# Moving work between the branches of a switched expert loop, with the gate on another engine

## The chip, the core and the metric

The kernel runs on one core of one Trainium2 chip. The metric is device time in microseconds (us) for one launch; three runs of the kernel before gave 488.0, 491.76 and 497.99, and their median counts. Engines are named TensorE (PE in the profile; PEld is its weight load), VectorE (DVE), ScalarE (ACT), GpSimd (POOL) and SyncE (SP, which here only issues transfers).

## The reference

A recurrent attention block is followed by a mixture of experts in which each token goes to one expert. All data are 32-bit floats.

```python
# q, k, v: (4, 8, 768, 64)
state = zeros(B, H, D, D)
for t in range(S):
    state = gamma[h] * state + outer(k[:, :, t], v[:, :, t])
    y[:, :, t] = scale * q[:, :, t] @ state
x = y.transpose(0, 2, 1, 3).reshape(3072, 512)

idx  = argmax(x @ w_gate, axis=1)               # 8 experts
gate = softmax(x @ w_gate)[idx]
for e in range(8):                              # w1: 512 x 1024, w2: 1024 x 512 per expert
    rows = idx == e
    y[rows] = maximum(x[rows] @ w1[e], 0) @ w2[e]
out = gate[:, None] * y
```

How many tokens an expert has is known only on the chip.

## The kernel before

Up to about 150 us the kernel runs the attention block and the routing; the change does not touch how that is done, but for where some registers are loaded. Then come eight **jobs**, one for each expert, 0 to 7. Job 0 and a first part of job 1 (256 tokens, `EARLY`) are done apart. A job takes its tokens, transposed, in `xTs` (512 features by up to `W` = 512 tokens), multiplies by `w1`, takes the positive part into `hT` (1024 features), and multiplies by `w2` into `yT`.

**Arms.** A job's width is a number of tokens in steps of 8. `tc.Switch(which, ARMS, ...)` holds 33 bodies, the **arms**, one for each width from 256 to 512, and a register that was loaded from the counts picks one. TensorE, ScalarE and VectorE have instructions in the arms of jobs 1 to 7 and so branch there; GpSimd and SyncE have none and run straight through. `regs` loads the register on each branching engine (it shows as line 515, `TENSOR_LOAD arm`). `fetch_ahead` (line 519) is a hint to TensorE and ScalarE, not to VectorE, which arm the next Switch will take. Between two arms lies what is here called a **seam**: the engine leaves one arm, loads the register, and enters the next.

**The two layers.** Each layer is computed as seven products of quarters instead of eight, on half the job's width: tokens are split in two interleaved halves, so every product has `n // 2` columns, and sums and differences of operands and of results replace the eighth product. For a job: `S` (four tiles, the sums of quarters of `w1`, line 283) and `Z` (the same of `w2`, line 299) are made by GpSimd; `T` (sums of `xTs`, line 315) and `G` (sums of `hT`, line 381) by VectorE. `quarters1` (products at line 333) runs twice seven products, for two pairs of f; in each pair the order is ya, yb, yd, yc, ya, yd, yc. ya, yb, yc, yd are accumulators; after the first ya ScalarE copies it to `m1` (line 345); VectorE then adds yb to m1 into `u2`, yd to u2 into `u3` (line 337), and further results to these. The second ya, yd, yc products add to the buffers that hold the first ones. `quarters2` (products at line 395, adds at line 399) is the same for layer 2: A(0,0) and A(0,1), then Sq(2), Sq(3), Sq(1), and as its **last two products** A(1,1) by `G[3]` into yd and Sq(4) into yc.

**Between the products.** `spare1` in layer 1 has VectorE turn the former job's `yT` back into rows (`turn_back`, line 444); `spare2` in layer 2 has it turn the next job's tokens into `xTs` (line 438) and make `T`.

**At the seam, outside the arms**, in program order: `finish(e - 1)` sends the former job's rows from `yg` to `o` by SyncE (`exchange`, line 433, 16 transfers), GpSimd multiplies them by the gate (line 1125, four instructions) and scatters them to the output (line 500, four indirect transfers). Then GpSimd makes `S` for the next job, SyncE loads `w1` for the job after it (2 MB), exchanges that job's tokens and loads its `w2` (2 MB), and GpSimd gathers tokens of the third next job (line 171) and makes `Z`. Each engine runs its own stream in this order, held by semaphores where it needs another's result; so GpSimd makes S for the next job while TensorE is in the arm of the present one. After job 7 its remaining part (256 tokens) is done by `pair` (lines 455 to 484), with no Switch.

## Time and profile before

| | |
|---|---|
| Runs | 488.0, 491.76, 497.99 us; median 491.76 us |
| Profiled execution | 487.66 us, of it 485.9 us span |
| Mean granted TensorE clock | 0.951 |
| Busy, share of the span | TensorE 89%, VectorE 51%, ScalarE 24%, GpSimd 61% |
| TensorE idle ahead of line 333 | 35.2 us, 28.4 of it "issue" |
| GpSimd's gate, line 1125 | 45.4 us in 24 instructions |
| S on GpSimd, line 283 | 2.3 us for each of four |
| Instructions fetched (queues q8, q14) | 48 and 68 packets, 0.79 and 0.56 MB |

A row of a timeline has the start in us, the duration, engine, line, operation, the written tile and the read ones, and in brackets how long the engine stood idle before and what ended it. "issue" stands where it waited for nothing that the profile shows. A row of the groups ends with busy us, mean ns of one instruction, and the idle time ahead of the group with its main releaser. A row of the waits gives the total, how often, and the longest. The rows of TensorE with "x8" are one product for two f (f0 and f0 + 1), those with "x16" one product of layer 2 for both d, and "x32" the two ya products of layer 2; the number behind "128x" is the half width of the job. Jobs 1 to 7 had 196, 196, 212, 176, 208, 180 and 204 columns here.

### The profile page before, as it was taken

How to read it: one execution, taken by the hardware profiler on the slowest of the kernel's cores; microseconds unless marked ns; L12 is line 12 of the kernel's file. 1: busy time of each engine (PE TensorE's matmuls, PEld its weight loads, DVE VectorE, ACT ScalarE, POOL GpSimd, SP SyncE). 2: the span in 40 equal slices, each digit the busy share in tenths (PEclk: the TensorE clock that was granted, in tenths of full speed). 3: DMA queues.
4: the chain of work that ended last, by engine and by line, in shares of the span. 5: the costliest groups of instructions: out<-in, count | busy, mean ns of one | idle time of the engine just before them, and what ended most of it. 6: DMA issues, size and time to landing. Idle time of an engine off the chain costs nothing.

```text
span 485.9 us, 9701 instructions
## 1 busy us (share of the span) xinstructions
PE 430.5 (89%) x3595; PEld 394.1 (81%) x3595; DVE 246.9 (51%) x554; ACT 115.9 (24%) x269; POOL 296.8 (61%) x224
## 2 busy tenths in 40 slices
PE   6899999996999999859978996799599959959993
PEld 4688888885888699859968996799599859959872
DVE  4445768694689505424833482356067415815510
ACT  3355544542212122003201310130023003102310
POOL 3575545505073294257799599929996990797451
PEclk9999999997999999979997999799899979999997
DMA  9999999999414747948667457448746543011221
GB/s 198 237 230 212 236 239 211 231 240 375 122 41 128 288 113 238 396 88 275 209 180 236 92 206 211 144 94 280 229 120 206 154 172 77 27 62 39 52 87 48
DMA packets 122116, 85.33 MB, mean 176 GB/s; under 512 B 56970, under 2 KB 106122, under 8 KB 122000
## 3 DMA queue, kind: packets, MB, share of 16 engines
q1 hardware_dynamic: 116736, 71.34, 54.1%
q0 software_dynamic: 5120, 12.60, 7.8%
q8 instruction: 48, 0.79, 0.7%
q14 instruction: 68, 0.56, 0.4%
q10 hardware_dynamic: 144, 0.05, 0.0%
HBM read 60.88 MB, written 14.68 MB: 156 GB/s over the span
## 4 chain that ended last, share of the span: by engine, by line
PE 59%; DMA 13%; SPq 11%; issue 8%; DVE 5%; POOL 1%; ACT 1%; POOLq 0%; DVEq 0%; ACTq 0%
PE p L333 21%; PE p L395 8%; SPq L433 7%; PE p L230 6%; DMA w1t<-in_moe_w_dram 5%; PE y L681 4%; PE p L243 3%; PE hp L230 3%; PE sc L627 3%; DMA k<-in_k_dram 3%; PE p L455 2%; DMA w2t<-in_moe_w_dram 2%; DMA xs<-xs 2%; SPq L576 2%; PE trq L595 2%
## 5 line engine op out<-in xcount | busy, mean ns | idle before, releaser
L333 PE MATMUL p<-xTs,w1t 128*128 128x196 f32 (+5 forms) x192 | 44.1, 382 | 35.2 <-issue 28.4
L1125 POOL TENSOR_SCALAR o<-o,gate 128x512 f32<-128x512 f32 x24 | 45.4, 1904 | 46.2 <-DMA o<-o 27.7
L333 PEld LDWEIGHTS p<-xTs,w1t 128*128 128x128 f32 x192 | 38.5, 223 | 37.0 <-issue 36.8
L444 DVE STREAM_TRANSPOSE o<-yT 128x512 f32<-128x512 f32 x24 | 16.8, 699 | 59.4 <-issue 28.9
L171 POOL DMA_INDIRECT xs<-x_d,src x28 | 30.5, 1088 | 26.0 <-issue 12.6
L631 DVE TENSOR_TENSOR am<-sc,causal 128x512 f32<-128x512 f32 x48 | 30.0, 684 | 20.0 <-PE sc L627 19.9
L589 POOL TENSOR_TENSOR vs<-v,dec 128x512 f32<-128x512 f32 x23 | 25.3, 1117 | 23.7 <-DMA v<-in_v_dram 21.7
L333 PE MATMUL p<-t,s 128*128 128x196 f32 (+5 forms) x192 | 39.6, 354 | 0.0
L345 ACT COPY q<-p 128x196 f32<-128x196 f32 (+5 forms) x24 | 7.7, 322 | 130.1 <-PE p L333 130.1
L337 DVE TENSOR_TENSOR hT<-p,q 128x196 f32<-128x196 f32 (+5 forms) x72 | 25.2, 356 | 26.0 <-PE p L333 25.8
L500 POOL DMA_INDIRECT out_dram<-o,dst x26 | 27.3, 1052 | 16.3 <-ACT o L251 9.5
L333 PEld LDWEIGHTS p<-t,s 128*128 128x128 f32 x192 | 36.9, 212 | 0.2
L333 PE MATMUL p<-t,w1t 128*128 128x196 f32 (+5 forms) x192 | 35.8, 329 | 0.0
L395 PE MATMUL p<-g,w2t 128*128 128x196 f32 (+4 forms) x192 | 33.6, 328 | 0.0
L395 PE MATMUL p<-g,z 128*128 128x196 f32 (+4 forms) x192 | 33.6, 328 | 0.0
L584 POOL TENSOR_TENSOR qs<-q,dec 128x512 f32<-128x512 f32 x22 | 22.3, 1042 | 17.3 <-DMA q<-in_q_dram 15.6
L395 PE MATMUL p<-hT,w2t 128*128 128x196 f32 (+4 forms) x192 | 32.6, 328 | 0.0
L333 PEld LDWEIGHTS p<-t,w1t 128*128 128x128 f32 x192 | 32.6, 191 | 0.0
L395 PEld LDWEIGHTS p<-g,z 128*128 128x128 f32 x192 | 31.9, 190 | 0.0
L395 PEld LDWEIGHTS p<-g,w2t 128*128 128x128 f32 x192 | 31.9, 190 | 0.0
L395 PEld LDWEIGHTS p<-hT,w2t 128*128 128x128 f32 x192 | 31.7, 190 | 0.0
L681 PE MATMUL y<-am,vs 128*64 128x128 f32 x384 | 25.3, 286 | 3.8 <-POOL vs L589 3.8
(217 smaller groups left out, 856.9 us busy)
## 6 DMA issues: line engine op xcount, KB each, us to landing
w1t<-in_moe_w_dram SPq DMA_DIRECT2D x7, 2048.0 KB
w2t<-in_moe_w_dram SPq DMA_DIRECT2D x7, 2048.0 KB
k<-in_k_dram SPq DMA_DIRECT2D x24, 256.0 KB
v<-in_v_dram SPq DMA_DIRECT2D x24, 256.0 KB
x_d<-xg SPq DMA_DIRECT2D x48, 128.0 KB
xs<-xs SPq DMA_DIRECT2D x96, 64.0 KB
o<-o SPq DMA_DIRECT2D x96, 64.0 KB
q<-in_q_dram SPq DMA_DIRECT2D x11, 512.0 KB
```

Source lines behind the costliest of these rows:

```text
L171: nc.gpsimd.indirect_dma_start(out=xs[:, t, :], out_offset=None, in_=x_d[0:rows, :], in_offset=bass.IndirectOffsetOnAxis(ap=idx[:, t : t + ...
L230: nc.tensor.matmul(hp, lhsT=w1t[:, 0, dt, ts(f, P)], rhs=xT[:, dt, n0:n], start=(dt == 0), stop=(dt == DT - 1))
L333: nc.tensor.matmul(rows(y), lhsT=a(d, f), rhs=b(d), start=start and d == 0, stop=d == 1, skip_group_check=True)
L337: nc.vector.tensor_tensor(out=to, in0=rows(y), in1=rows(plus), op=ALU.add)
L395: nc.tensor.matmul(rows(y), lhsT=a(f, d), rhs=b(f), start=start and f == 0, stop=f == FH - 1, skip_group_check=True)
L433: nc.sync.dma_start(to[ts(g, L), :, ts(r, P)], got[ts(r, L), :, ts(g, P)])
L500: done = nc.gpsimd.indirect_dma_start(out=out[:, :], out_offset=bass.IndirectOffsetOnAxis(ap=idx[:, t : t + 1], axis=0), in_=o[:, t, :], i ...
L584: by.tensor_tensor(out=qs[:, e, part, :], in0=got[:, part, ts(e, D)], op=ALU.mult, in1=inner(dec[:, ts(2 * where[s][0] + e, H)][:, part], D))
L589: by.tensor_tensor(out=vs, in0=raw.pop(("v", s, b)), op=ALU.mult, in1=inner(dec[:, ts(NC + 2 * where[s][0] + where[s][2], H)], D))
L631: nc.vector.tensor_tensor(out=am[j], in0=sc[j], in1=middle(causal[:, :], HP), op=ALU.mult)
L681: nc.tensor.matmul(place_of(y, b, a, j), lhsT=vs[:, 2 * a + j, :], rhs=am[b][0][j][:, a, :], start=alone, stop=True, skip_group_check=True)
L1125: nc.gpsimd.tensor_scalar(out=yg[:, t, :].rearrange("p (a g l) -> p a g l", g=Q, l=L), in0=o[:, t, :].rearrange("p (g a l) -> p a g l", g= ...
```

## The change

A constant `SEAM` of 216 columns is introduced, and the products take a range of columns `c`.

- The last two products of layer 2, with their adds, leave the arm: `last2` runs them after the Switch for columns 0 to 216, whatever the width, and the arm only what lies above 216 (nothing for jobs of up to 432 tokens).
- The first product of the next job's layer 1, for both f, and its copy to `m1` (`first1`) leave the next arm in the same way and stand behind `last2`.
- The gate moves from GpSimd to ScalarE, as an activation with a scale.
- The registers of jobs 2 to 7 are loaded in the layer-1 loop of job 1 (f = 1 to 6), not one at each seam; that of job 1 is loaded behind the one of job 0.
- The hint for the next Switch stands behind the arm, ahead of `last2`, not ahead of layer 2 within the arm. Job 1's stays where it was.
- On GpSimd a copy of one column of `T[3]` into `turn_of` is put ahead of `S`, so `S` starts after `T[3]` is made; and the gather stands behind `Z`. The clearing of `yT` is cut to its upper columns, and those of `hT`, `G[3]` and `u2` are cleared as well, since the fixed width reads past the job's.

```diff
+    SEAM = 216
+    def last2(hT, w2t, S, T, yT, temps, c):
+        yc, yd = (acc8[i : i + 2] for i in (2, 4))
+        u2 = temps[1]
+        Y = lambda i, k, d: part_of(yT[:, 2 * i + d, :], k, c)
         for d in range(2):
-            product(yd[d], A(1, 1), Tq(4), d, False)
-            add(Y(1, 0, d), yd[d], u2[d])
+            products(yd[d], [(quarter_of_w2(w2t, 1, 1)[:, f, ts(d, P)], columns(T[3][:, f, :], c)) for f in range(FH)],
+                     c, False)
+            adds(Y(1, 0, d), columns(yd[d], c), columns(u2[d], c))
         for d in range(2):
-            product(yc[d], Sq(4), X(1, 1), d, False)
-            add(Y(0, 1, d), yc[d], u2[d])
+            products(yc[d], [(S[3][:, f, ts(d, P)], part_of(hT[:, FH + f, :], 1, c)) for f in range(FH)], c, False)
+            adds(Y(0, 1, d), columns(yc[d], c), columns(u2[d], c))
...
+    def first1(xT, w1t, f, ya, m1, c):
+        products(ya, [(w1t[:, 0, d, ts(f, P)], part_of(xT[:, d, :], 0, c)) for d in range(2)], c, c[0] == 0)
+        nc.scalar.copy(out=m1[:, c[0] : c[1]], in_=ya[:, c[0] : c[1]])
...
             for t in range(TC):
-                nc.gpsimd.tensor_scalar(out=yg[:, t, :].rearrange("p (a g l) -> p a g l", g=Q, l=L),
-                                        in0=o[:, t, :].rearrange("p (g a l) -> p a g l", g=Q, l=L),
-                                        scalar1=cols[e][2][:, t : t + 1], scalar2=None, op0=ALU.mult)
+                nc.scalar.activation(out=yg[:, t, :].rearrange("p (a g l) -> p a g l", g=Q, l=L),
+                                     in_=o[:, t, :].rearrange("p (g a l) -> p a g l", g=Q, l=L), func=AF.Copy,
+                                     scale=cols[e][2][:, t : t + 1])
             scatter(yg, cols[e][1], range(TC))
...
+        for f in range(FT):
+            layer1(EARLY, xT1, w1s[1], hT, f, banks=(2, 3, 4, 5, 0, 1))
+            if f == 0:
+                fetch_ahead(which[1], 1)
+            elif f < E - 1:
+                which[f + 1] = regs(f + 1)
...
-                fetch_ahead(nxt, e + 1)
-                quarters2(n, hT, w2s[e], Z, G, yT, temps, spare2)
+                quarters2(hT, w2s[e], Z, G, yT, temps, spare2, (0, n // 2))
+                if n // 2 > SEAM:
+                    last2(hT, w2s[e], Z, G, yT, temps, (SEAM, n // 2))
...
             if e > 1:
                 finish(e - 1)
-            S = halves_of_w1(w1s[e + 1], s3)
+            fetch_ahead(which[e + 1], e + 1)
+            last2(hT, w2s[e], Z, G, yT, temps, (0, SEAM))
+            for f in range(2):
+                first1(xTs, w1s[e + 1], f, acc8[6 + f], temps[0][f], (0, SEAM))
             if e + 2 < E:
                 w1s.append(weights1(homes[e % 2], e + 2))
                 exchange(xg, xs)
                 w2s.append(weights2(homes[e % 2], e + 2))
-            if e + 3 < E:
-                gather(xs, cols[e + 3][0], range(TC))
+            nc.gpsimd.tensor_copy(turn_of, T[3][:, 0, 0:1])
+            S = halves_of_w1(w1s[e + 1], s3)
             if e + 1 < E - 1:
                 Z = halves_of_w2(w2s[e + 1], z3)
...
+            if e + 3 < E:
+                gather(xs, cols[e + 3][0], range(TC))
```

**The seam on TensorE and VectorE.** The rows show the seam between jobs 1 and 2. What stands ahead of it in the stream is the widest arm (256 columns), what follows is the narrowest (128); the p are accumulators, g is `G`, z is `Z`. On TensorE, before:

```order
L395 MATMUL p_2338<-g_2355,w2t 128x256 x4
L395 MATMUL p_2339<-g_2355,w2t 128x256 x4
L395 MATMUL p_2336<-hT,z_2347 128x256 x4
L395 MATMUL p_2337<-hT,z_2347 128x256 x4
L1237 UNCONDITIONAL_BRANCH
L515 TENSOR_LOAD arm
L515 ISA x2
L1237 SWITCH_STRIDE
L1237 ISA x2
L1152 BRANCH_PREFETCH_HINT
L333 MATMUL p_2340<-xTs,w1t 128x128 x2
L333 MATMUL p_2341<-xTs,w1t 128x128 x2
```

The same place on TensorE in the changed kernel:

```order
L1259 UNCONDITIONAL_BRANCH
L535 SWITCH_STRIDE
L535 ISA
L535 BRANCH_PREFETCH_HINT
L330 MATMUL p_2365<-g_2382,w2t 128x216 x4
L330 MATMUL p_2366<-g_2382,w2t 128x216 x4
L330 MATMUL p_2363<-hT,z_2374 128x216 x4
L330 MATMUL p_2364<-hT,z_2374 128x216 x4
L330 MATMUL p_2367<-xTs,w1t 128x216 x2
L330 MATMUL p_2368<-xTs,w1t 128x216 x2
L1259 SWITCH_STRIDE
L1259 ISA x2
```

Between leaving (the unconditional branch) and entering (the second `SWITCH_STRIDE` with its `ISA`) there stood a register load; now there stand the hint and six rows of products.

VectorE at this seam in the changed kernel (yT is layer 2's result, o_2355 is `yg`, the q are m1, u2 and u3):

```order
L1259 UNCONDITIONAL_BRANCH
L334 TENSOR_TENSOR yT<-p_2365,q_2389 128x54x4
L334 TENSOR_TENSOR yT<-p_2366,q_2390 128x54x4
L334 TENSOR_TENSOR yT<-p_2363,q_2389 128x54x4
L334 TENSOR_TENSOR yT<-p_2364,q_2390 128x54x4
L1259 SWITCH_STRIDE
L1259 ISA x2
L1171 BRANCH_PREFETCH_HINT
L460 STREAM_TRANSPOSE o_2355<-yT 128x512
L334 TENSOR_TENSOR q_2389<-p_2361,q_2387 128x128
L334 TENSOR_TENSOR q_2390<-p_2362,q_2388 128x128
L460 STREAM_TRANSPOSE o_2355<-yT 128x512
```

The four adds of the moved products stand between the two branches, where VectorE had the register load alone; no hint stands ahead of its entry.

**The gate, ScalarE and GpSimd.** The rows show the seam between jobs 2 and 3. ScalarE in the changed kernel, from the last copies of an arm on:

```order
L417 COPY yT<-p_2367 128x64x4
L417 COPY yT<-p_2368 128x64x4
L1259 UNCONDITIONAL_BRANCH
L1147 ACTIVATE o_2355<-o_2356,gate 128x512 x4
L535 SWITCH_STRIDE
L535 ISA
L535 BRANCH_PREFETCH_HINT
L339 COPY q_2387<-p_2367 128x216
L339 COPY q_2388<-p_2368 128x216
L1259 SWITCH_STRIDE
L1259 ISA x2
```

The gate, the hint and the two copies of the moved first product stand between its branches. GpSimd at this seam, before:

```order
L1125 TENSOR_SCALAR o_2328<-o_2329,gate 128x512 x4
L500 DMA out_dram<-o_2328,dst 3072x512 x4
L283 TENSOR_TENSOR s_2342<-w1t 128x1024
L283 TENSOR_TENSOR s_2343<-s_2342,w1t 128x1024
L283 TENSOR_TENSOR w1t<-w1t 128x2x512
L283 TENSOR_TENSOR s_2344<-w1t,s_2343 128x1024
L171 DMA xs_112<-x_d,src 128x512 x4
L299 TENSOR_TENSOR z_2345<-w2t 128x1024
```

And in the changed kernel:

```order
L516 DMA out_dram<-o_2355,dst 3072x512 x4
L1219 COPY turn_of<-t_2378 128x1
L283 TENSOR_TENSOR s_2369<-w1t 128x1024
L283 TENSOR_TENSOR s_2370<-s_2369,w1t 128x1024
L283 TENSOR_TENSOR w1t<-w1t 128x2x512
L283 TENSOR_TENSOR s_2371<-w1t,s_2370 128x1024
L299 TENSOR_TENSOR z_2372<-w2t 128x1024
L299 TENSOR_TENSOR z_2373<-z_2372,w2t 128x1024
L299 TENSOR_TENSOR w2t<-w2t 128x4x256
L299 TENSOR_TENSOR z_2374<-w2t,z_2373 128x1024
L1259 UNCONDITIONAL_BRANCH
L171 DMA xs_112<-x_d,src 128x512 x4
```

The gate rows are gone, the copy that reads `T[3]` (t_2378) stands ahead of S, and the gather has moved past Z.

More of the change, by code (lines that the diff above doesn't have):

```diff
@@ L342, in quarters1 @@
             m1, u2, u3 = temps
+            lo = done if f0 == 0 else 0
             for i, f in enumerate(fs):
-                product(ya[i], A(0, 0), X(0, 0), f, True)
-                nc.scalar.copy(out=m1[i][:, 0:m], in_=ya[i][:, 0:m])
+                if m > lo:
+                    first1(xT, w1t, f, ya[i], m1[i], (lo, m))
             spare()
@@ L348, in quarters1 @@
                 product(yb[i], Sq(2), Tq(2), f, True)
-                add(rows(u2[i]), yb[i], m1[i])
+                adds(columns(u2[i], c), columns(yb[i], c), columns(m1[i], c))
             spare()
@@ L352, in quarters1 @@
                 product(yd[i], Sq(3), Tq(3), f, True)
-                add(rows(u3[i]), yd[i], u2[i])
+                adds(columns(u3[i], c), columns(yd[i], c), columns(u2[i], c))
             spare()
@@ L356, in quarters1 @@
                 product(yc[i], Sq(1), Tq(1), f, True)
-                add(H(1, 1, f), yc[i], u3[i])
+                adds(H(1, 1, f), columns(yc[i], c), columns(u3[i], c))
             spare()
@@ L367, in quarters1 @@
                 product(yc[i], Sq(4), X(1, 1), f, False)
-                add(H(0, 1, f), yc[i], u2[i])
+                adds(H(0, 1, f), columns(yc[i], c), columns(u2[i], c))
                 nc.scalar.activation(out=H(0, 1, f), in_=H(0, 1, f), func=AF.Relu)
@@ L381, in sums_of_h, with quarters2 @@
             nc.vector.tensor_tensor(out=out_, in0=a, in1=b, op=ALU.subtract)
-    def quarters2(n, hT, w2t, S, T, yT, temps, spare):
-        m, nb = n // 2, n // 8
-        rows = lambda ap: in_four(ap, m)
-        X = lambda j, k: lambda f: by_halves(hT[:, j * FH + f, :])[:, k, 0:nb, :]
+    def quarters2(hT, w2t, S, T, yT, temps, spare, c):
+        X = lambda j, k: lambda f: part_of(hT[:, j * FH + f, :], k, c)
         A = lambda i, j: lambda f, d: quarter_of_w2(w2t, i, j)[:, f, ts(d, P)]
-        Y = lambda i, k, d: by_halves(yT[:, 2 * i + d, :])[:, k, 0:nb, :]
+        Y = lambda i, k, d: part_of(yT[:, 2 * i + d, :], k, c)
         Sq = lambda i: lambda f, d: S[i - 1][:, f, ts(d, P)]
-        Tq = lambda i: lambda f: rows(T[i - 1][:, f, :])
+        Tq = lambda i: lambda f: columns(T[i - 1][:, f, :], c)
         def product(y, a, b, d, start):
-            for f in range(FH):
-                nc.tensor.matmul(rows(y), lhsT=a(f, d), rhs=b(f), start=start and f == 0, stop=f == FH - 1,
-                                 skip_group_check=True)
-        def add(to, y, plus):
-            nc.vector.tensor_tensor(out=to, in0=rows(y), in1=rows(plus), op=ALU.add)
+            products(y, [(a(f, d), b(f)) for f in range(FH)], c, start)
         ya, yb, yc, yd = (acc8[i : i + 2] for i in (6, 0, 2, 4))
@@ L404, in quarters2 @@
             product(ya[d], A(0, 0), X(0, 0), d, True)
-            nc.scalar.copy(out=m1[d][:, 0:m], in_=ya[d][:, 0:m])
+            nc.scalar.copy(out=columns(m1[d], c), in_=columns(ya[d], c))
         for d in range(2):
             product(ya[d], A(0, 1), X(1, 0), d, False)
-            nc.scalar.copy(out=Y(0, 0, d), in_=rows(ya[d]))
+            nc.scalar.copy(out=Y(0, 0, d), in_=columns(ya[d], c))
         spare()
@@ L411, in quarters2 @@
             product(yb[d], Sq(2), Tq(2), d, True)
-            add(rows(u2[d]), yb[d], m1[d])
+            adds(columns(u2[d], c), columns(yb[d], c), columns(m1[d], c))
         spare()
@@ L415, in quarters2 @@
             product(yd[d], Sq(3), Tq(3), d, True)
-            add(rows(u3[d]), yd[d], u2[d])
+            adds(columns(u3[d], c), columns(yd[d], c), columns(u2[d], c))
         spare()
@@ L951, in within_early @@
         def within_early(f):
-            nonlocal ne, arm, src, far, which
+            nonlocal ne, arm, src, far
             if f == 1:
@@ L1153 @@
+        xT = xT1
+        for e in range(1, E):
+            last = e + 1 == E
+            for a in tc.Switch(which[e], ARMS, hint=f"job{e}"):
                 n = STEP * (LEAST + a)
@@ L1206 @@
                 halves_of_w(w2s[e + 1], z4, by=nc.gpsimd)
-            xT, which = xTn, nxt
+            if e + 3 < E:
+                gather(xs, cols[e + 3][0], range(TC))
+            xT = xTs
         e = E - 1
```

106 lines of the change are left out of this document (51 added, 55 removed).

## The prediction

> **What bounds the kernel now.** I read the page's busy line and its groups first, then the waits of TensorE from 150 us on, then the timelines of the engines around one seam (the stretch in which one job's arm is left and the next one's is entered). From 150 us to the end TensorE never waits for data, except at the seams:
>
> ```profile
> span 485.9 us, 9701 instructions
> PE 430.5 (89%) x3595; PEld 394.1 (81%) x3595; DVE 246.9 (51%) x554; ACT 115.9 (24%) x269; POOL 296.8 (61%) x224
> ...
> PE p L333 <- issue: 28.4, 5, 7.0
> PE p L333 <- DMA xs<-xs: 6.9, 1, 6.9
> PE p L230 <- DVE xTa L214: 0.3, 1, 0.3
> ```
>
> The last three rows are all waits of TensorE in that stretch: total, times, longest. Six pauses, 28.4 + 6.9 = 35.3 us, stand ahead of line 333, five of them put down to "issue": nothing the profile shows was waited for. The timeline of TensorE shows them as the first products of jobs 2 to 7, and gives the widths of the jobs:
>
> ```profile
> 164.77 21.39 PE L230 MATMUL p<-xT,w1t 128*128 128x256 f32 x128
> ...
> 199.26 2.82 PE L395 MATMUL p<-g,w2t 128*128 128x196 f32 x16
> 201.91 2.82 PE L395 MATMUL p<-hT,z 128*128 128x196 f32 x16
> 211.59 2.95 PE L333 MATMUL p<-xTs,w1t 128*128 128x196 f32 x8 [6.86 <-DMA xs<-xs]
> ...
> 232.84 5.47 PE L395 MATMUL p<-hT,w2t 128*128 128x196 f32 x32
> ...
> 246.11 2.82 PE L395 MATMUL p<-g,w2t 128*128 128x196 f32 x16
> ...
> 256.52 3.17 PE L333 MATMUL p<-xTs,w1t 128*128 128x212 f32 x8 [4.94 <-issue]
> 306.25 2.68 PE L333 MATMUL p<-xTs,w1t 128*128 128x176 f32 x8 [7.03 <-issue]
> 346.31 2.85 PE L333 MATMUL p<-xTs,w1t 128*128 128x208 f32 x8 [5.04 <-issue]
> 394.04 2.74 PE L333 MATMUL p<-xTs,w1t 128*128 128x180 f32 x8 [6.42 <-issue]
> 435.20 2.94 PE L333 MATMUL p<-xTs,w1t 128*128 128x204 f32 x8 [4.92 <-issue]
> ```
>
> The six brackets sum to 35.2 us. The first row is the counter-example: it holds the eight early products of job 1 and, in the same group, those of the arm of job 1; there the hint stands outside the arm with seven products behind it, and TensorE enters the arm without a pause. So a pause is not the price of every entry; it is what is left when nothing covers it.
>
> A pause costs more than itself. The page has three groups of line 333 with the same count and the same six widths:
>
> ```profile
> L333 PE MATMUL p<-xTs,w1t 128*128 128x196 f32 (+5 forms) x192 | 44.1, 382 | 35.2 <-issue 28.4
> L333 PE MATMUL p<-t,s 128*128 128x196 f32 (+5 forms) x192 | 39.6, 354 | 0.0
> L333 PE MATMUL p<-t,w1t 128*128 128x196 f32 (+5 forms) x192 | 35.8, 329 | 0.0
> ...
> 209.00:216.00 7.00, 4.41 (x14) 4.44 (x15) 0.75 (x2) 0.64 (x2) 3.84 (x2) 0.58 0.23 54
> 216.00:232.00 16.00, 16.00 (x95) 16.00 (x94) 7.96 (x21) 4.25 (x11) 10.74 (x7) 0.97 0.79 234
> ```
>
> The first group holds the product right behind each pause, the second the next one, the third none of them: (44.1 - 35.8) + (39.6 - 35.8) = 12.1 us are lost to slow products. The stretches behind them (columns after the busy times: granted clock, DMA share, GB/s) give the reason: the clock is 0.58 where work comes back and 0.97 afterwards. [...]
>
> **The change, part by part.** *Removed on TensorE:* if the pauses go entirely, 35.2 + 12.1 = 47.3 us.
>
> *Extra columns.* Two 16-matmul groups of layer 2 and one 8-matmul group of layer 1 now always have 216 columns. A 16-group of 196 columns takes 201.91 - 199.26 = 2.65 us, 13.5 ns a column. Layer 2 of jobs 1 to 6 (196, 196, 212, 176, 208, 180) lacks 128 columns of 6 x 216: 2 x 128 x 13.5 ns = 3.5 us. Layer 1 of jobs 2 to 7 lacks 120: 120 x 6.75 ns = 0.8 us. Together **+4.3 us**. This work is the cover: 216 columns make 2 x 2.92 + 1.46 = 7.3 us between the arms, against pauses of 4.9 to 7.0.
>
> *Registers and hints.* One register load a seam leaves TensorE, ScalarE and VectorE, and six stand between job 1's early products, inside the 21.39 us row. Today's load stands right ahead of that row and left no gap there; I take 0, and up to 3 us if VectorE or ScalarE are held up by six of them. The hint no longer stands ahead of layer 2 inside the arm, but 7.3 us ahead of the entry outside it, as in job 1. I take entry on TensorE as free there; its cost if not is the third rival.
>
> *VectorE is late next.* It has no hint before or after, and its pauses are longer than TensorE's:
>
> ```profile
> 214.40 0.71 DVE L444 STREAM_TRANSPOSE o<-yT 128x512 f32<-128x512 f32 x1 [9.27 <-ACT q L345]
> ...
> 262.41 0.71 DVE L444 STREAM_TRANSPOSE o<-yT 128x512 f32<-128x512 f32 x1 [10.43 <-DMA w2t<-in_moe_w_dram]
> 263.05 0.62 DVE L337 TENSOR_TENSOR q<-p,q 128x212 f32<-128x212 f32 x2
> 263.60 0.69 DVE L444 STREAM_TRANSPOSE o<-yT 128x512 f32<-128x512 f32 x1
> 264.21 0.62 DVE L337 TENSOR_TENSOR q<-p,q 128x212 f32<-128x212 f32 x2
> ...
> 311.19 0.71 DVE L444 STREAM_TRANSPOSE o<-yT 128x512 f32<-128x512 f32 x1 [11.55 <-issue]
> 352.45 0.71 DVE L444 STREAM_TRANSPOSE o<-yT 128x512 f32<-128x512 f32 x1 [10.80 <-DMA w2t<-in_moe_w_dram]
> 398.85 0.71 DVE L444 STREAM_TRANSPOSE o<-yT 128x512 f32<-128x512 f32 x1 [10.82 <-issue]
> 437.23 0.71 DVE L444 STREAM_TRANSPOSE o<-yT 128x512 f32<-128x512 f32 x1 [6.57 <-issue]
> ```
>
> Count from the end of the arm's last product. TensorE runs the moved products to 7.3 us, then four 8-groups of the new arm (4.8 to 5.7 us by width); the fifth, yd's second product, adds into the buffer that VectorE's first u3 add reads. From entry VectorE needs 264.5 - 262.4 = 2.1 us to finish that add. So it must be in by 10.4, 10.8, 9.9, 10.7, 10.0 and 10.6 us. When does it come? Its last add of the arm starts at 0.25, the whole old pause (leave, load, enter) then counts, and four adds of 0.36 lie within: 0.25 + pause + 1.44 gives 11.0, 12.1, 13.2, 12.5, 12.5 and 8.3, too late by 9.5 us in sum. The other end is nothing: the sixth pause, with no register load in it, is 6.57; half of it to leave and half to enter puts the entry at 6.1 (start of the last moved add) + 3.3 = 9.4, in time everywhere. The load goes from five pauses, but nothing shows how much of them it was. I take the middle, **+5 us**, with ends 0 and 9.5.
>
> *ScalarE's gate and GpSimd.* Line 1125 leaves GpSimd and frees it from 45.4 us of work. On ScalarE it starts only when the arm is left:
>
> ```profile
> L1125 POOL TENSOR_SCALAR o<-o,gate 128x512 f32<-128x512 f32 x24 | 45.4, 1904 | 46.2 <-DMA o<-o 27.7
> L1116 ACT ACTIVATE o<-ident 128x512 f32<-128x512 f32 x2 | 1.1, 622 | 4.6 <-DVE gate L205 4.6
> ...
> 165.02 0.69 ACT L251 ACTIVATE o<-p,gate 104x512 f32<-104x512 f32 x1 [6.66 <-DVE over L542]
> 168.57 0.83 ACT L232 ACTIVATE hT<-p 128x256 f32<-128x256 f32 x2 [2.87 <-issue]
> ...
> 238.35 0.32 ACT L408 COPY yT<-p 128x196 f32<-128x196 f32 x1 [1.00 <-PE p L395]
> ...
> 203.49 2.33 POOL L283 TENSOR_TENSOR s<-w1t 128x1024 f32<-128x1024 f32 x1 [9.43 <-DMA w1t<-in_moe_w_dram]
> 205.90 2.34 POOL L283 TENSOR_TENSOR s<-s,w1t 128x1024 f32<-128x1024 f32 x1
> ...
> 244.77 1.40 POOL L500 DMA_INDIRECT out_dram<-o,dst  x1 [0.17 <-POOL o L1125]
> ...
> 249.07 0.98 POOL L500 DMA_INDIRECT out_dram<-o,dst  x1 [0.30 <-issue]
> 250.06 2.37 POOL L283 TENSOR_TENSOR s<-w1t 128x1024 f32<-128x1024 f32 x1
> ```
>
> Behind the waiting gate stand ScalarE's hint and the two copies of the moved first product; behind the scatters stand GpSimd's S, then Z and the gather, moved past them. For job 2: ScalarE is done in the arm at 238.7, leaves it in 2.9 us (as after job 0), gates 4 x 0.62 to 244.1; the scatters, 250.06 - 244.77 = 5.3 us from the first gate on, end near 247.5; two steps of S (4.7 us) give S[1] at 252.2. The arm there ends at 246.1 (its last two groups of 2.65 us, moved out, ended at 251.4), and the new arm's first product wants S[1] at 246.1 + 7.3 = 253.4: 1.2 us to spare. I take 0 for five seams; with a leave of 5.8 us (half of VectorE's longest pause) it is 1.7 x 5 = 8.5. The new copy on GpSimd that waits for T[3] is short, and T is done before the scatters are. The first seam is different: S waits for a weight load until 203.49 and S[1] is ready at 205.90 + 2.34 = 208.2, while TensorE would ask at 199.26 + 7.3 = 206.6: **+1.6 us**, not seen today because the pause covers it. At the end, job 6's gates (2.5 us) stand ahead of ScalarE's last products' copies and delay the scatters: **+1**, from 0 to 3.
>
> **Sum.** 487.7 - 47.3 + 4.3 + 5 + 1.6 + 1 = 452.3 us against the profiled execution's 487.66. That execution lies below all runs shown (488.0 to 497.99, median 491.76, +0.8%); I carry half of the difference and say **454 us**.
>
> **The rivals.** *Nothing waits at all.* VectorE comes in time, the rest as above: 487.7 - 47.3 + 4.3 + 1 = 446; for it speaks the sixth pause, against it the five others.
>
> *VectorE becomes the bound.* Its leave is as short as ScalarE's 2.87 and the rest of its pause is the entry, which starts only with the last moved add at 6.1: entry at 12.5, 13.7, 14.8, 14.0, 14.1, 9.8, late by 16.8 us in all; and stalls of 3 to 5 us give back part of the slow clock, up to half of 12.1. 487.7 - 47.3 + 4.3 + 16.8 + 1.6 + 1 + 3 = 467. Against it: the register load was part of the pause.
>
> *The pause stays.* Entering costs TensorE what it does now, because the target's code must be brought in whatever is hinted, or because the entry waits for the queue to run empty: 487.7 + 4.3 = 492, less whatever part was the load, so 480 to 492, no change. Against it stands the 21.39 us row. [...]
>
> *The gate on ScalarE holds up the seam (slower).* ScalarE leaves the arm only with the others: at the arm's end, 13.3 us into layer 2 (232.84 + 13.3 = 246.1 in job 2), plus VectorE's 11.55, so at 24.9. From leaving to S[1] go 0.6 + 5.3 + 4.7 = 10.6 us, and S[1] is wanted at 20.6: 15 us late at five seams, 446 + 75 = 521. It makes the kernel slower than before from a leave at about 18.5 us on, where each seam loses over 8.5 us beside the slow clock. Against it: after job 0 ScalarE left its arm alone, in 2.87 us.
>
> **How the numbers follow.** Forecast (448 to 461) 0.54; nothing waits 0.14; VectorE the bound (461 to 478) 0.17; the pause stays 0.09; slower by the gate 0.06. The range 442 to 475 holds the first three but for the tail of the third: the low end is 446 less the 3.8 us by which the lowest run lies under the median, the high one is 452.3 with VectorE's other end (+4.5), the gate's 8.5, 2 more at the end, 3 for registers and the median's whole distance of 4.1. A change under 2% can't be told from none in this kernel: faster needs under 482. One hundredth of the fourth case is faster still, one of the last no change: **faster 0.86, same 0.09, slower 0.05.**
>
> **What would show it.** Waits of TensorE: no bracket of 5 to 7 us at the seams, at most some of 1 to 3 ahead of yd's second product, released by VectorE; one of about 1.6 us at the first seam, released by GpSimd. The groups of layer 1 equal in mean duration, the clock above 0.9 at the seams. GpSimd's busy time 45 us lower, ScalarE's about 15 higher (24 x 0.62). I am wrong if TensorE still waits for "issue" behind the moved products, if VectorE's first transpose comes later than 11 us after the arm's end, or if the scatters end after S is wanted.

## The result, and the profile after

The changed kernel took 468.65 us (median of four runs, 464.4 to 470.01) against 490.5 for the kernel before in the same comparison: a ratio of 0.9563, with a 95% interval of 0.9485 to 0.964. It is faster by 4.4%. The forecast of 454 us was 15 us too low, inside its range of 442 to 475; the sign and the main mechanism held, but of the 37.8 us that it promised on the median (491.76 to 454) only 21.9 came. In later comparisons the same code stood at 0.9539 [0.9434, 0.9644] and 0.9509 [0.9456, 0.9563]. Some executions of one kernel are longer as a whole (in experiment 9 one took 477.96 us, the other five 466.58 to 470.52); they are left out of the ratios and of the differences between kernels, but not of the medians listed.

The page of the profiled execution (464.4 us), its span, its busy line and three groups of layer 1 that answer to those shown of before:

```profile
span 462.7 us, 9728 instructions
PE 426.4 (92%) x3595; PEld 388.3 (84%) x3595; DVE 245.7 (53%) x554; ACT 131.0 (28%) x293; POOL 249.4 (54%) x210
...
L330 PE MATMUL p<-t,s 128*128 128x196 f32 (+5 forms) x192 | 37.1, 338 | 7.5 <-POOL w1t L283 4.2
L330 PE MATMUL p<-t,w1t 128*128 128x196 f32 (+5 forms) x192 | 36.8, 335 | 4.2 <-DVE q L334 2.5
L330 PE MATMUL p<-xTs,w1t 128*128 128x216 f32 (+6 forms) x192 | 36.6, 333 | 0.0
```

The 35.2 us of idle time have become 7.5 + 4.2 = 11.7. The group with no pause ahead of it took 35.8 us before; the two others, of the jobs' own widths, now take 37.1 and 36.8, so 2.3 us of the 12.1 us of slow products are left. GpSimd's busy time fell from 296.8 to 249.4 us, ScalarE's rose by 15.1, both as forecast. TensorE's timeline shows the pauses that remain (all rows with a bracket at the seams; between them the start of job 1, some of the moved products and the last product of all):

```profile
166.61 21.39 PE L230 MATMUL p<-xT,w1t 128*128 128x256 f32 x128
...
213.11 2.70 PE L330 MATMUL p<-t,s 128*128 128x196 f32 x8 [4.15 <-POOL w1t L283]
215.61 2.07 PE L330 MATMUL p<-t,w1t 128*128 128x196 f32 x8
...
245.38 3.08 PE L330 MATMUL p<-g,w2t 128*128 128x216 f32 x16
248.30 3.08 PE L330 MATMUL p<-hT,z 128*128 128x216 f32 x16
...
254.33 1.67 PE L330 MATMUL p<-t,s 128*128 128x212 f32 x8 [1.48 <-POOL s L283]
256.55 1.70 PE L330 MATMUL p<-t,w1t 128*128 128x212 f32 x8 [0.55 <-POOL w1t L283]
...
288.18 3.08 PE L330 MATMUL p<-g,w2t 128*128 128x216 f32 x16
...
302.91 1.46 PE L330 MATMUL p<-t,w1t 128*128 128x176 f32 x8 [2.49 <-DVE q L334]
335.03 1.65 PE L330 MATMUL p<-t,s 128*128 128x208 f32 x8 [1.87 <-POOL s L283]
337.25 1.67 PE L330 MATMUL p<-t,w1t 128*128 128x208 f32 x8 [0.58 <-POOL w1t L283]
...
413.05 1.65 PE L330 MATMUL p<-t,w1t 128*128 128x204 f32 x8 [0.55 <-POOL w1t L283]
...
449.01 1.89 PE L471 MATMUL p<-w2t,g 128*128 128x256 f32 x8
```

At the third, fifth and sixth seam TensorE passes from the moved products into the next arm without a gap. At the second and fourth the first product of the arm waits 1.48 and 1.87 us, but it starts 0.15 us after `S[1]`, which it reads, is ready (254.18 and 334.88 us), and in experiment 11, where `S` comes sooner, both gaps are gone. The other pauses come a product or more later and are another engine's too. So five of six entries cost TensorE nothing of their own here; only the first seam has a pause of the old kind, whatever its label (experiments 7 and 10). From the start of job 1 to the end of TensorE's work the changed kernel needs 450.9 - 166.6 = 284.3 us, the kernel before needed 477.5 - 164.8 = 312.7: 28.4 us less. I compare this stretch below, since the start of job 1 itself moves from one execution of the same code to the next: 166.61 here, 173.99 and 168.55 in the two later profiles.

How S becomes late, in the timelines of ScalarE (first two rows) and GpSimd at the seam between jobs 2 and 3:

```profile
237.62 0.32 ACT L417 COPY yT<-p 128x196 f32<-128x196 f32 x1 [1.00 <-PE p L330]
243.04 2.56 ACT L1147 ACTIVATE o<-o,gate 128x512 f32<-128x512 f32 x4 [5.10 <-issue]
...
244.04 1.35 POOL L516 DMA_INDIRECT out_dram<-o,dst  x1 [14.66 <-ACT o L1147]
...
249.41 2.35 POOL L283 TENSOR_TENSOR s<-w1t 128x1024 f32<-128x1024 f32 x1
251.84 2.34 POOL L283 TENSOR_TENSOR s<-s,w1t 128x1024 f32<-128x1024 f32 x1
```

ScalarE is done in its arm at 237.9 and begins the gate 5.10 us later, having waited in between for nothing that the profile shows. The scatters follow, then S; S[1] is ready at 254.18, and TensorE's first row in the new arm starts at 254.33.

The end is longer: TensorE's last product ends 11.8 us ahead of the end of the span (before: 8.4). ScalarE and GpSimd there:

```profile
441.57 2.56 ACT L1147 ACTIVATE o<-o,gate 128x512 f32<-128x512 f32 x4 [2.04 <-issue]
...
442.57 0.99 POOL L516 DMA_INDIRECT out_dram<-o,dst  x1 [17.88 <-ACT o L1147]
...
454.27 0.98 POOL L516 DMA_INDIRECT out_dram<-yT,dst  x1 [4.28 <-issue]
```

And one row of the chain of waits there:

```profile
442.57 10.32 DMA out_dram<-o,dst
```

The first scatter of job 6 is issued at 442.57, after 17.88 us of waiting for ScalarE's gate; the chain puts 10.3 us on these transfers, and the last two scatters are issued only after that. In the kernel before and in experiment 11 the chain runs over TensorE's products to the end instead.

### The profile page after: what moved, and what is told of

Same layout as the page of the kernel before. It is cut to its first block, busy times and chain, and to the rows that moved or that the text cites. A ratio compares the mean times of both kernels' runs of the same rounds, so it can differ in the third digit from the quotient of the medians.

```text
span 462.7 us, 9728 instructions
## 1 busy us (share of the span) xinstructions
PE 426.4 (92%) x3595; PEld 388.3 (84%) x3595; DVE 245.7 (53%) x554; ACT 131.0 (28%) x293; POOL 249.4 (54%) x210
## 4 chain that ended last, share of the span: by engine, by line
issue 27%; PE 22%; POOL 20%; DMA 16%; SPq 8%; DVE 3%; ACT 1%; POOLq 1%; ACTq 0%; DVEq 0%
POOL s L283 7%; DMA k<-in_k_dram 6%; POOL xs L171 4%; POOL out_dram L516 4%; PE p L230 4%; DMA xs<-xs 4%; SPq L449 3%; PE hp L230 3%; POOL z L299 3%; SPq L592 2%; PE y L697 2%; DMA out_dram<-o,dst 2%; PE sc L643 2%; PE trq L611 2%; PE p L330 2%
## 5 line engine op out<-in xcount | busy, mean ns | idle before, releaser
L330 PE MATMUL p<-t,s 128*128 128x196 f32 (+5 forms) x192 | 37.1, 338 | 7.5 <-POOL w1t L283 4.2
L330 PE MATMUL p<-t,w1t 128*128 128x196 f32 (+5 forms) x192 | 36.8, 335 | 4.2 <-DVE q L334 2.5
L330 PEld LDWEIGHTS p<-t,s 128*128 128x128 f32 x192 | 33.2, 194 | 8.4 <-issue 8.4
L334 DVE TENSOR_TENSOR hT<-p,q 128x196 f32<-128x196 f32 (+5 forms) x72 | 24.9, 355 | 28.4 <-PE p L330 23.6
L605 POOL TENSOR_TENSOR vs<-v,dec 128x512 f32<-128x512 f32 x23 | 23.8, 1049 | 29.5 <-DMA v<-in_v_dram 27.7
L171 POOL DMA_INDIRECT xs<-x_d,src x28 | 28.8, 1029 | 19.4 <-issue 13.2
L334 DVE TENSOR_TENSOR q<-p,q 128x196 f32<-128x196 f32 (+5 forms) x72 | 24.6, 351 | 26.0 <-PE p L330 24.3
L330 PE MATMUL p<-xTs,w1t 128*128 128x216 f32 (+6 forms) x192 | 36.6, 333 | 0.0
L330 PE MATMUL p<-g,w2t 128*128 128x216 f32 (+5 forms) x192 | 35.4, 338 | 0.1
L330 PEld LDWEIGHTS p<-xTs,w1t 128*128 128x128 f32 x192 | 33.1, 190 | 0.0
L460 DVE STREAM_TRANSPOSE o<-yT 128x512 f32<-128x512 f32 x24 | 16.8, 699 | 26.9 <-issue 10.7
L600 POOL TENSOR_TENSOR qs<-q,dec 128x512 f32<-128x512 f32 x22 | 22.3, 1042 | 16.2 <-DMA q<-in_q_dram 15.3
L334 DVE TENSOR_TENSOR yT<-p,q 128x216 f32<-128x216 f32 (+5 forms) x36 | 12.6, 371 | 32.4 <-PE p L330 25.3
L377 ACT ACTIVATE hT<-p 128x196 f32<-128x196 f32 (+5 forms) x24 | 7.9, 333 | 68.7 <-PE p L330 59.2
```

The lines of the kernel that those rows point to most:

```text
L171: nc.gpsimd.indirect_dma_start(out=xs[:, t, :], out_offset=None, in_=x_d[0:rows, :], in_offset=bass.IndirectOffsetOnAxis(ap=idx[:, t : t + ...
L330: nc.tensor.matmul(columns(y, c), lhsT=a, rhs=b, start=start and i == 0, stop=i + 1 == len(terms), skip_group_check=True)
L334: nc.vector.tensor_tensor(out=to, in0=y, in1=plus, op=ALU.add)
L460: nc.vector.transpose(to[:, t, :].rearrange("p (r a l) -> p r a l", r=Q, l=L), got[:, :, ts(t, P)].rearrange("p a (r i) -> p r a i", i=L))
L600: by.tensor_tensor(out=qs[:, e, part, :], in0=got[:, part, ts(e, D)], op=ALU.mult, in1=inner(dec[:, ts(2 * where[s][0] + e, H)][:, part], D))
L605: by.tensor_tensor(out=vs, in0=raw.pop(("v", s, b)), op=ALU.mult, in1=inner(dec[:, ts(NC + 2 * where[s][0] + where[s][2], H)], D))
```

## The experiments

Two theories stood against each other at each place; ratios are to the kernel before run beside it, and "stretch" is from the start of job 1 to TensorE's end in the profiled execution.

| Kernel | Median us | Ratio [95%] | Stretch | End |
|---|---|---|---|---|
| before | 490.5 to 496.1 | 1 | 312.7 | 8.4 |
| changed | 468.65 | 0.9563 [0.9485, 0.964] | 284.3 | 11.8 |
| 1 products in the arm | 489.73 | 0.9915 [0.9873, 0.9956] | 307.5 | 12.2 |
| 2 hint in the arm | 478.65 | not given | 294.1 | 11.7 |
| 3 registers at the seam | 472.38 | 0.9559 [0.9472, 0.9647] | 288.9 | 12.1 |
| 4 gate on GpSimd | 467.4 | 0.9452 [0.9397, 0.9507] | 288.1 | 8.8 |
| 5 changed, again | 470.18 | 0.9539 [0.9434, 0.9644] | 282.5 | 11.9 |
| 6 S ahead of the scatters | 473.56 | 0.9659 [0.9526, 0.9792] | 291.6 | 11.8 |
| 7 w1 first | 465.59 | 0.9483 [0.9375, 0.9591] | 282.2 | 11.8 |
| 8 hint for VectorE | 468.47 | 0.9465 [0.9334, 0.9597] | 285.4 | 11.9 |
| 9 changed, again | 468.54 | 0.9509 [0.9456, 0.9563] | 285.2 | 11.9 |
| 10 loads held | 464.86 | 0.9456 [0.9401, 0.9512] | 282.1 | 11.9 |
| 11 gate shared | 459.87 | 0.9348 [0.9298, 0.9398] | 278.7 | 8.4 |
| 12 both | 460.01 | 0.9329 [0.9269, 0.9388] | 279.7 | 8.4 |

**1. The moved products back in the arms.**

```diff
                 quarters2(hT, w2s[e], Z, G, yT, temps, spare2, (0, n // 2))
-                if n // 2 > SEAM:
-                    last2(hT, w2s[e], Z, G, yT, temps, (SEAM, n // 2))
+                last2(hT, w2s[e], Z, G, yT, temps, (0, n // 2))
...
-            last2(hT, w2s[e], Z, G, yT, temps, (0, SEAM))
-            for f in range(2):
-                first1(xTs, w1s[e + 1], f, acc8[6 + f], temps[0][f], (0, SEAM))
```

In layer 1 the argument that skips the moved columns goes too.

> The changed kernel, but with the last two products of layer 2 and the first of layer 1 back in the arms at the job's own width. Registers early, hint outside the arm, gate on ScalarE stay. Theory (the entry of an arm takes its time and the moved products hide it): TensorE has pauses of 3 to 6 us again at all six seams, 20 to 35 us in sum, with slow products behind them (8 to 12 us), less 4.3 us of extra columns: 480 to 492 us. Rival (the register load at the seam was the pause): the pauses stay gone, 458 to 466 us.

The waits of TensorE from 150 us on:

```profile
PE p L330 <- issue: 16.5, 5, 5.0
PE p L330 <- DVE q L334: 9.3, 3, 4.2
PE p L330 <- DMA xs<-xs: 3.1, 1, 3.1
```

Six pauses are back, 16.5 + 3.1 = 19.6 us instead of 35.2, and VectorE is late behind three of them for 9.3 more. The theory's time came (489.73, ratio 0.9915): what is left of the change (early registers, hint outside the arm, gate on ScalarE) shortens TensorE's pauses by 15.6 us, but VectorE, the next one late, takes 9.3 of it back, and the longer end 3.8. Without the moved products nearly nothing of the change's gain is left.

**2. The hint back inside the arm.**

```diff
+                fetch_ahead(which[e + 1], e + 1)
                 quarters2(hT, w2s[e], Z, G, yT, temps, spare2, (0, n // 2))
...
-            fetch_ahead(which[e + 1], e + 1)
             last2(hT, w2s[e], Z, G, yT, temps, (0, SEAM))
```

> The changed kernel, but with the hint back inside the arm, ahead of layer 2; the moved products stay outside. Theory (a hint that is given before the arm is left does not serve the next entry, as the pauses of before show): TensorE pauses of 2 to 5 us at each seam behind the moved products, together 12 to 30 us: 478 to 495 us. Rival (7.3 us of products hide the entry, whatever was hinted): no more pauses than in the changed kernel, 464 to 470 us.

Its four runs lie far apart (478.13, 479.18, 479.84 and 465.61), and the profile is of one of the three long ones, so it shows only what can happen. TensorE's rows there:

```profile
208.30 3.19 PE L330 MATMUL p<-g,w2t 128*128 128x216 f32 x16 [3.03 <-issue]
...
251.10 4.87 PE L330 MATMUL p<-g,w2t 128*128 128x216 f32 x16 [4.11 <-issue]
```

The pauses without a releaser stand ahead of the moved products, where the arm is left, not behind them, where the next is entered. Neither of my theories had that. The run of 465.61 is as short as the changed kernel's, as the rival has it, and no profile shows it; so it stays open whether the place of the hint matters.

**3. Registers at the seam again.**

```diff
-                which[f + 1] = regs(f + 1)
...
             if e + 2 < E:
+                which[e + 2] = regs(e + 2)
                 w1s.append(weights1(homes[e % 2], e + 2))
```

The register of job 2 is still loaded in the loop of job 1, those of jobs 3 to 7 at the five seams ahead of the last.

> The changed kernel, but with one register load at each seam again (behind the first moved product, ahead of the entry), on TensorE, ScalarE and VectorE. Theory (the loads are hidden on TensorE by the moved products, and only VectorE enters later): 0 to 1.5 us more at each of five seams, 464 to 474 us, the pauses released by VectorE. Rival (the load made most of the old pause): TensorE pauses of 3 us and more with no releaser at each seam, 480 us and more.

Of TensorE's waits:

```profile
PE p L330 <- DVE q L334: 6.0, 3, 3.3
```

The ratio is that of the changed kernel. TensorE waits for VectorE 6.0 us in three pauses (there 2.5 in one); the only pause without a releaser is the 3.49 us of the first seam. As the theory has it, the register loads are hidden on TensorE and VectorE enters later: 7.56 and 7.10 us at the second and fifth seam, where it took 3.25 and 3.24 in the changed kernel.

**4. The gate on GpSimd again.**

```diff
-                nc.scalar.activation(..., func=AF.Copy, scale=cols[e][2][:, t : t + 1])
+                nc.gpsimd.tensor_scalar(..., scalar1=cols[e][2][:, t : t + 1], scalar2=None, op0=ALU.mult)
```

> The changed kernel, but with the gate on GpSimd again. GpSimd can begin it when the exchanged rows have landed, 1 to 5 us into layer 2, and needs 6.8 to 8.8 us for it; ScalarE began 8 to 11 us into layer 2, when it had left the arm, and needed 2.6. Theory (leaving the arm costs ScalarE what its quicker gate gains): S starts within 2 us of where it does in the changed kernel, the same pauses put down to S (5 us), and an end that is 3 us shorter, since job 6's scatters no longer wait for ScalarE: 460 to 468 us. Rival (the gate on ScalarE is what lets S come in time): S 4 us later at five seams, 20 us more: 480 to 488 us.

GpSimd at the seam between jobs 2 and 3, and from TensorE's waits the row on S:

```profile
241.18 6.86 POOL L1147 TENSOR_SCALAR o<-o,gate 128x512 f32<-128x512 f32 x4 [7.31 <-DMA o<-o]
248.21 1.07 POOL L516 DMA_INDIRECT out_dram<-o,dst  x1 [0.17 <-POOL o L1147]
```

```profile
PE p L330 <- POOL s L283: 8.8, 3, 3.8
```

The pauses put down to S grow from 5.0 (the short ones labelled w1t among them) to 9.7 (8.8, and 0.9 labelled w1t), the end shrinks from 11.8 to 8.8. The time and the end are the theory's, the pauses for S are not: they are twice what it had, at three seams, far from the rival's 20 us. On the whole this kernel is not slower than the changed one: moving the gate to ScalarE brought about 4 us at the seams and lost 3 at the end.

**5 and 9. The changed kernel again**, beside 6 to 8 and 10 to 12.

> The changed kernel itself, unchanged, as the yardstick for the three that run beside it. Both theories: 0.95 to 0.965 of the kernel before. Pauses of TensorE at the seams 9 to 14 us in sum: 3.5 to 4.2 at the first seam, 1.5 to 2.5 at the second and fourth, released by S, 2.5 at the third, released by VectorE.

> The changed kernel itself, as the yardstick for the three beside it. Both theories: 0.945 to 0.965 of the kernel before, a pause of 3.5 to 4.2 us at the first seam, an end of 11 to 12 us between TensorE's last product and the end of the span.

The ratios came in both, and of the second all that was expected. In the first VectorE was in time at the third seam, against what I had written, and the pauses of TensorE at the seams sum to 8.2 us, below the 9 to 14; in the second TensorE waited 1.7 us for VectorE there.

**6. S ahead of the scatters, not held back.**

```diff
+            if not last:
+                S = halves_of_w1(w1s[e + 1], s3)
             if e > 1:
                 finish(e - 1)
...
-            nc.gpsimd.tensor_copy(turn_of, T[3][:, 0, 0:1])
-            S = halves_of_w1(w1s[e + 1], s3)
```

> The changed kernel, but GpSimd makes S ahead of the scatters, and without the copy that holds it back until T[3] is made. Theory (the pauses at seams 2, 4 and 6 come from scatters that wait for ScalarE to leave its arm and stand ahead of S): these pauses, 5 us in sum, go, and nothing else changes: 4 to 6 us less than the unchanged kernel run beside it. Rival (S beside VectorE's sums of layer 2 slows these, which is why the copy holds S back): VectorE's sums (0.97 and 0.69 us now) take 1.2 to 1.7, and TensorE waits for them inside layer 2; no gain, or up to 5 us more.

VectorE's sums of layer 2 and GpSimd's S beside them, in this kernel:

```profile
236.24 3.01 DVE L397 TENSOR_TENSOR g<-hT,g 128x784 f32<-128x784 f32 x1
239.17 3.12 DVE L397 TENSOR_TENSOR g<-hT 128x784 f32<-128x784 f32 x1
...
235.25 3.16 POOL L283 TENSOR_TENSOR w1t<-w1t 128x1024 f32<-128x1024 f32 x1
```

And from TensorE's waits:

```profile
PE p L330 <- DVE t L315: 4.6, 2, 3.6
PE p L330 <- DVE g L397: 4.0, 6, 1.5
```

The rival came, and harder than I wrote: of VectorE's four sums of a job two take 3.0 to 3.1 us instead of 0.97, a little less than their own time and one of GpSimd's steps together (0.97 + 2.35), and GpSimd's third step of S takes 3.16 instead of 2.35. The pauses for S are gone, but TensorE waits 4.0 us for the sums of hT and 4.6 for T; the stretch is 6 to 9 us longer. Making S beside these sums costs more than it brings; the run does not tell the copy that holds S back from S's place behind the scatters, since both were changed. The sum that starts at 236.24 ends at 239.25, 0.8 us after GpSimd's step beside it does (235.25 + 3.16 = 238.41); what holds it up no row shows.

**7. w1 of job 2 loaded ahead of its w2.**

```diff
-        w2s.append(weights2(homes[0], 2))
         w1s.append(weights1(homes[0], 2))
+        w2s.append(weights2(homes[0], 2))
```

> The changed kernel, but after job 0 the load of w1 for job 2 is issued ahead of that of w2. Theory A (the 4.15 us pause at the first seam is S, which waits for w1 until 205.5): w1 lands 4 to 6 us sooner, S is ready in time, the pause falls under 1 us: 4 to 6 us less. Theory B (that pause is the entry of the arm itself, slow while 4 MB of weights come in): S starts sooner but the pause of 3.5 to 4 us stays, put down to issue: 0 to 1 us less.

GpSimd's second step of S, and TensorE at the first seam:

```profile
204.38 2.36 POOL L283 TENSOR_TENSOR s<-s,w1t 128x1024 f32<-128x1024 f32 x1
...
214.40 2.01 PE L330 MATMUL p<-t,s 128*128 128x196 f32 x8 [3.92 <-POOL z L299]
```

S[1] is ready at 206.7, 3.7 us before the pause begins, and the pause is still 3.92 us. So the first seam's pause is not S; the bracket names a step of Z, done at 213.6 us, which this product does not read. That leaves the entry, theory B. The median is 4.6 us below the changed kernel's beside it, but the intervals overlap and the stretches are the same (282.2 and 282.5).

**8. The hint for VectorE too.**

```diff
-        tc.switch_hint({g: which[g] for g in (PE, ACT)}, ARMS, label=f"job{e}")
+        tc.switch_hint({g: which[g] for g in which}, ARMS, label=f"job{e}")
```

> The changed kernel, but the hint for the next arm goes to VectorE too. Theory (VectorE enters late because nothing prepares its entry): its pauses of 6 to 7.5 us at seams 1 and 3 fall to 3.3 and under, and TensorE's 2.5 us behind it go: 2 to 4 us less. Rival (its entry takes 3 us hinted or not, and the longer ones come from transfers beside it, as ScalarE's hinted entries of 2.3 to 5.2 us suggest): pauses of 3 to 7 us as now, no change within 1 us.

VectorE's first row in the arms of jobs 2 and 6:

```profile
218.86 0.71 DVE L460 STREAM_TRANSPOSE o<-yT 128x512 f32<-128x512 f32 x1 [6.29 <-issue]
...
383.29 0.71 DVE L460 STREAM_TRANSPOSE o<-yT 128x512 f32<-128x512 f32 x1 [6.53 <-DMA w2t<-in_moe_w_dram]
```

With 5.68 us for job 4 they are as long as in the changed kernel, some longer (there 7.49, 6.22 and 3.24 for jobs 2, 4 and 6): the rival came, and VectorE gains nothing that shows from the hint.

**10. Loads held back from the first seam** (with the order of experiment 7).

```diff
-                w1s.append(weights1(homes[e % 2], e + 2))
+                if e > 1:
+                    w1s.append(weights1(homes[e % 2], e + 2))
                 exchange(xg, xs)
                 w2s.append(weights2(homes[e % 2], e + 2))
+                if e == 1:
+                    w1s.append(weights1(homes[e % 2], e + 2))
```

> The changed kernel with two orders of loads changed: after job 0 the w1 of job 2 goes ahead of its w2, and at the first seam the w2 of job 3, which has to wait until layer 2 of job 1 is done with its buffer, goes ahead of the w1 of job 3, so that this load of 2 MB does not run while the first seam is passed. Theory (the first seam's pause is the entry, slow while transfers fill all queues: DMA share 1.02 there, 0.5 to 0.85 at the others): the share at the entry falls and the pause of 3.9 us falls to 0 to 1.5, with the slow products behind it: 3 to 6 us less. Rival (the first entry is slow for another reason, such as that it is the first into these arms): the pause stays at 3 to 4 us.

Two windows about the first entry in this kernel (the last columns are granted clock, DMA share and GB/s), then the timelines of TensorE at the first two seams, of GpSimd's second step of S ahead of the first, and of SyncE's exchange ahead of the second gate:

```profile
202.00:206.00 4.00, 4.00 (x24) 4.00 (x23) 0.61 (x3) 0.00 (x0) 3.92 (x3) 1.00 0.57 184
206.00:210.00 4.00, 2.78 (x17) 2.48 (x15) 0.74 (x3) 0.68 (x2) 4.00 (x3) 1.00 0.34 79
```

```profile
209.97 1.56 PE L330 MATMUL p<-t,s 128*128 128x196 f32 x8 [1.22 <-POOL s L283]
...
203.03 2.35 POOL L283 TENSOR_TENSOR s<-s,w1t 128x1024 f32<-128x1024 f32 x1
...
253.28 3.17 PE L330 MATMUL p<-t,s 128*128 128x212 f32 x8 [5.25 <-POOL s L283]
...
217.65 23.13 SPq L449 DMA_DIRECT2D o<-o  x16
```

The same windows, and the same places of the timelines, in the unchanged kernel beside it:

```profile
202.00:206.00 4.00, 4.00 (x24) 3.81 (x23) 0.79 (x3) 0.00 (x0) 0.19 (x1) 1.00 1.04 405
206.00:210.00 4.00, 4.00 (x24) 4.00 (x23) 1.15 (x4) 0.00 (x0) 2.27 (x1) 1.00 1.01 399
```

```profile
214.69 2.69 PE L330 MATMUL p<-t,s 128*128 128x196 f32 x8 [4.03 <-issue]
...
221.70 16.20 SPq L449 DMA_DIRECT2D o<-o  x16
```

With a share of 0.34 to 0.57 instead of 1.01 to 1.04 the pause falls from 4.03 to 1.22 us. S is not in it, whatever the label: `S[1]` was ready at 205.38, 3.4 us before the pause began; in experiment 12 the same place has 1.12 us put down to "issue". Experiment 7 has the same order of the first two loads and S in time as well, but the load not held, and there the pause was 3.92, with a share of 1.01 to 1.12 from 198 to 212. So at this seam the pause of the entry was 3.9 to 4.0 us where the transfers were at full share ahead of it, and 1.1 to 1.2 us where they were at 0.34 to 0.57. VectorE's entry at this seam goes with it, 2.91 us here against 6.83. But the held load comes back at the next seam: it stands ahead of the exchange, which takes 23.1 us instead of 16.2, the gate waits for it, and S is 5.25 us late there. Together the stretch is 3.1 us shorter, where three executions of the changed kernel differ by 2.7 (282.5 to 285.2), and the two intervals overlap.

**11. The gate shared, and on GpSimd alone after the last arm.**

```diff
-            for t in range(TC):
+            gp = TC if end else TC // 2
+            for t in range(gp):
+                nc.gpsimd.tensor_scalar(...)
+            scatter(yg, cols[e][1], range(gp))
+            for t in range(gp, TC):
                 nc.scalar.activation(...)
-            scatter(yg, cols[e][1], range(TC))
+            scatter(yg, cols[e][1], range(gp, TC))
```

`end` is true in the call behind the last arm alone.

> The changed kernel with the gate shared: GpSimd does two of four tiles, and scatters them, while ScalarE still leaves its arm, ScalarE does the other two; for job 6, after the last arm, GpSimd does all four. Theory (S is late because all four scatters wait for ScalarE to leave its arm; the end is long because job 6's scatters do): S starts 2 to 3 us sooner after layer 2 begins (14 to 17 us now), the pauses at seams 2, 4 and 6 (5 us in sum) fall to 0 to 1.5, and the end of 11.8 us to 8 to 9: 5 to 8 us less. Rival (GpSimd's gate slows VectorE as S did, and gives the gain back): TensorE waits for VectorE inside layer 2, the end alone is shorter: 0 to 3 us less.

All waits of TensorE at the seams:

```profile
PE p L330 <- POOL w1t L283: 4.2, 1, 4.2
PE p L330 <- DVE q L334: 2.9, 1, 2.9
```

The first row is the first seam's entry; the pauses for S at seams 2, 4 and 6 are gone, and the end is 8.4 us again. 459.87 us, 7.7 less than the unchanged kernel beside it, as the theory has it; the rival's cost does not show, and VectorE's sums take 0.97 us as before. ScalarE leaves its arm no sooner (4.97 us at the second seam); half of the scatters no longer wait for it.

**12. Loads held and gate shared.** Both edits above together.

> The changed kernel with the orders of loads and the shared gate of the two kernels beside it together. Theory: their gains add, 8 to 13 us less than the changed kernel, 0.93 to 0.94 of the kernel before; TensorE's pauses at the seams under 4 us in sum, what is left of them released by VectorE. Rival (the places are not independent, since what one gives the next engine takes): no better than the better of the two.

```profile
PE p L330 <- POOL s L283: 6.7, 1, 6.7
```

460.01 us: by this row of TensorE's waits the rival came. The held load makes S 6.7 us late at the second seam, and the gain of the first is gone. Experiments 11 and 12 can't be told apart, and 11 is the simpler; its interval ends at 0.9398 where the changed kernel's beside it begins at 0.9456.

## Why the prediction was right, and where it fell short

- **Removing the pauses** (47.3 us): right. Five entries cost nothing of their own, 11.7 of 35.2 us of pauses are left, and 2.3 of 12.1 us of slow products. Experiment 1 shows that the moved products are needed: the registers, the hint and the gate alone leave 19.6 us of pauses and nearly the old time.
- **Extra columns** (+4.3): right: a group of layer 2 with 216 columns takes 248.30 - 245.38 = 2.92 us, as taken.
- **VectorE** (+5, ends 0 and 9.5): one pause of 2.49 us at the third seam, where I had the longest (3.3). VectorE's entry there:

```profile
300.83 0.71 DVE L460 STREAM_TRANSPOSE o<-yT 128x512 f32<-128x512 f32 x1 [6.22 <-DMA w2t<-in_moe_w_dram]
```

  It came 300.83 - 288.18 = 12.65 us after the arm's end, against a limit of 9.9. The other late entry, at the first seam, hides behind TensorE's own. The reason I gave, no hint, was wrong: experiment 8. The traces point at the transfers instead. In the changed kernel's first profile the entry of 6.22 us at the third seam had a DMA share of 0.90 while VectorE waited, the other four behind the first seam, 3.22 to 3.46 us, a share of 0.52 and less; at the first seam holding a load took the entry from 6.83 to 2.91 (experiment 10). Only that seam was tested. In the rival with VectorE as the bound, the lateness adds up to 17.3 us by the limits I printed, not 16.8; nothing hangs on it.
- **The gate on ScalarE** (0, other end 8.5): the term that failed first. I took its leave as 2.87 us, from the one row after job 0; it took 5.10 at the seam shown and 2.5 to 5.0 at the other four. That row was a quiet place: its DMA share was 0.39, while in the same profile the stretch in which I let ScalarE leave job 2's arm (238.67 to 243.00) had 1.01. In the changed kernel the leaves of 5.10 and 5.03 us had a share of 0.99 and 0.96, those of 2.0 to 3.1 one of 0.55 and less. In the profile of experiment 9 the first scatter came latest at the same two seams: 1.17 and 0.46 us ahead of TensorE's first moved product, at the third, fifth and sixth 3.2 to 4.3. The pauses sum to 1.48 + 0.55 + 1.87 + 0.58 + 0.55 = 5.0 us. The chain itself (gate, scatters, S) was right, and experiment 11 removes exactly these.
- **The first seam** (+1.6 for S): S was late as I wrote, by 1.3 us (`S[1]` ready at 210.28, asked for at 208.96), but the first product of the arm started 2.8 us after that. The seam cost 4.15 and 1.8 of slow products ((2.70 + 2.07) - 2 x 1.49), from another cause. My third rival, an entry that costs what it did, is true at this one seam: its pause was 3.92 us with the transfers at full share (experiment 7) and 1.22 with a share of 0.34 to 0.57 (experiment 10).
- **Slow products behind short pauses** (3 in the rival with VectorE as the bound, none in the forecast): the seams of the kernel before had no pause under 4.9 us, so no run of that kernel shows what a shorter one costs, and both were estimates of mine. In the changed kernel the 4.15 us of the first seam were followed by 1.8 us of slow products, and a pause of 1.9 us at the fourth by almost none in one profile, by a product of 2.76 us instead of 1.57 in another (last section).
- **The end** (+1, up to 3): 3.4 us, since the scatters of job 6 wait for ScalarE, and the last ones are issued only when the chain's 10.3 us for these are over. Experiments 4 and 11 give it back.
- **Sum.** 452.3 + 5.0 + (4.15 + 1.8 - 1.6) - 2.5 + 2.4 = 461.6; the start of job 1, 1.8 us later than in the execution of before, makes 463.4 of 464.4. The median stands 4 us above its own profiled execution, twice what I had allowed. A time of 468.65 lies in the band that I gave to VectorE as the bound (461 to 478), but VectorE cost only 2.5 us; the time was made by the gate, the first seam and the end, of which the range held the gate and part of the end.
- **Signs of being wrong.** Two of the three that I named showed at some seams: a pause at the first seam that the later profiles put down to "issue" (3.62 and 4.03 us), and VectorE's first transpose 14.3 and 12.65 us after the arm's end at the first and third, where I had set 11. The granted clock was 0.57 behind the first pause, from 213 to 217 us, where I had said above 0.9.
